# Local and global attention with an expert layer: smaller load pieces, weight buffers of their own, masks by half rows, global scores in spare columns

## The chip, the cores and the metric

The kernel runs on one core of a Trainium2 chip. The time is the device time of one execution in microseconds; it is given as the median of several runs, and one further execution is taken with the hardware profiler.

## What is computed

Eight batches of attention with 8 heads of size 64, 512 local and 32 global positions, and then a layer that replaces 128 chosen rows of each batch. All data is float32.

```python
k_all = concat([k_g, k_l]); v_all = concat([v_g, v_l])
out_g = softmax(q_g @ k_all.T / 8) @ v_all              # 32 global queries see everything
s_ll  = where(|i - j| <= 32, q_l @ k_l.T / 8, -1e9)     # local queries: a band
out_l = softmax([q_l @ k_g.T / 8, s_ll]) @ [v_g, v_l]   # and the 32 global keys
x = concat([out_g, out_l])                              # 8 batches, 576 rows, 512 wide
scores = x @ w_gate                                     # one number for each row
top = the 128 rows of each batch with the highest scores
x[top] += sigmoid(scores[top]) * (relu(x[top] @ w1) @ w2)    # w1 512x1024, w2 1024x512
```

## The kernel before

**Steps.** A batch is six steps in the order L0, L1, G0, L2, G1, L3. An L step is 128 local queries of all heads, a G step one half of the keys for the 32 global queries. Queries and keys lie with the head's 64 values along the partitions, two heads on top of each other, and the keys of a local block are 128 columns: two of its own, one global block, one neighbour. One loop (line 709) goes over all 48 steps as a software pipeline, so that in iteration `i` TensorE (PE) does, in this order: the mask of step `i+1` (`opened`, L247), the products with the values of step `i-1` (`attend_mm`, L328, or L429 for G), what stands in the list `early` (below), the scores of step `i+1` (L266, or L387), the transposes of step `i`'s exponentials (`transp`, L308 or L303), and then a share of the expert layer. ScalarE (ACT) takes exponentials (L293) and copies the transposes from PSUM (L315, tile `pt`), VectorE (DVE) does maxima and divisions. All engines follow the order in which the program is written.

**Mask.** `opened` takes one of three two-bank PSUM tiles `s_ps` and writes the mask into it before the scores are added: for each of the two banks one bfloat16 product of a 128x128 identity and 128 rows of mask, 256 columns. Such a pair stands in each of the 32 L steps.

**Global scores.** After the last G step of a batch `g_score` (L466) sums four partial scores of each global row by a one-column product, and DVE copies the 32 sums. One step later `spread_g` (L477) turns them into a row, which ACT copies into the tile `r` (L478 to L485), and `spread` (L484) does so for the 512 local scores. All three are called from `early` and take their PSUM tile from `m_tile()`, which hands out two buffers `m_ps` in turn. The expert layer takes its tiles from there too: L541 turns the gathered rows, L574 is the first product, L586 turns its result (copied by ACT and DVE into `hTh` and `hTl`, L589 and L590), L603 is the second product, whose tile stays open over four pieces of work.

**Loads.** Every load is issued by SyncE (SP) through `put` (L116). `put` counts back over the loads issued before it, and once their sizes with its own pass `UNDER` = 2000 KB, it makes the new load wait for the one at which this happened. So no more than 2000 KB are under way. Of each batch there are 4 pieces of keys of 416 KB, 8 of values of 520 KB, 2 of queries of 512 KB and a small one. The 16 pieces of expert weights (256 KB each) come in between by the table `LOADW` (iteration: number) and go into the buffers `xe` (shared with the rows that the expert layer gathers), `ws`, `xTh`, `xTl`, `hTh`, `hTl`, which the expert layer needs later. By the table `SPLITS` each piece is split into a rounded part (DVE for w1, ACT for w2) and a remainder (GpSimd). The expert layer begins at iteration 12.

Of the kernel before, what the change touches and what calls it, by code (L numbers as in the profile page):

```python
# [7 lines left out]
FP32 = mybir.dt.float32  # L8
# [9 lines left out]
P = 128  # L18
B, H, SL, SG, D = 8, 8, 512, 32, 64
ST = SG + SL  # L20
DM = H * D
FF = 1024
NT = SL // P
NC = SL // 32
NPAIR = H // 2
# [4 lines left out]
KC = DM // P  # L30
MC = FF // P
NEG = -1.0e30
# [4 lines left out]
ORDER = (("L", 0), ("L", 1), ("G", 0), ("L", 2), ("G", 1), ("L", 3))  # L37
PER = len(ORDER)
RESTL, LATE = 2, 6
LOADW = {4: 4, 5: 4, 7: 5, 11: 3}  # L40
SPLITS = {9: 2, 10: 3, 11: 3, 13: 3, 14: 3, 15: 2}

GROUPS = ((0,), (1,), (2,), (3,), (4,), (5,), (6,), (7,))
FIRST = 12
APART = 12
RANKS0 = {1: 2, 2: 3}
RANKS = {1: 1, 2: 2, 3: 2}
UNDER = 2000

RATE, HELD, FILL = 2.05, 2.6, 2.6  # L50
LEFT = 2.7
# [19 lines left out]
def kernel(ctx, tc, qT, kT, qgT, vw, w1, w2, wg, wgg, const, edge, outs, cap):  # L71
# [17 lines left out]

    ne = edge.shape[1] - P  # L90
    cb = cst.tile([P, ne], BF16, name="cb")
    ident16 = cb[:, 0:P]
    mask = cb[:, P:].rearrange("p (a k) -> p a k", a=3)
    ident = cs[:, o:o + P]; o += P
    slot = cs[:, o:o + NST * P]; o += NST * P
    tokid = cs[:, o:o + NT + 1]; o += NT + 1
# [10 lines left out]

    loaded = {}
    under = []

    def put(out, in_):
        kb = 4
        for n in in_.shape:
            kb *= n
        kb //= 1024
        d_ = nc.sync.dma_start(out=out, in_=in_)  # L116
        sum_ = kb
        for e_, k_ in reversed(under):
            sum_ += k_
            if sum_ > UNDER:  # L120
                tc.add_manual_dep(d_.ins, e_.ins.name, mybir.DependencyInfo(mybir.DependencyClass.Sync, mybir.DependencyReason.DATA), reason="under")
                break
        under.append((d_, kb))
        return d_
# [5 lines left out]
        loaded[b] = (q_t, k_t, qg_t)  # L130

    def load_q(b, n):
        put(out=loaded[b][0][n], in_=qT[b, n])

    def load_k(b, pr):
        put(out=loaded[b][1][:, pr], in_=kT[b, :, pr])
# [32 lines left out]

    def load_v(b, t):  # L170
        vts[b, t] = vld.tile([P, 4, H, VD], FP32, name="v_t")
        for j in range(0, 4, 2):
            put(out=vts[b, t][:, j:j + 2], in_=vw[b, t, :, j:j + 2])

    end = {"on": False, "n": 0}

# [1 line left out]
    def m_tile():  # L178
        if end["on"]:
            end["n"] += 1  # L180
            if end["n"] % 5 in (0, 1, 3):
                return ps_s.tile([P, 2, 512], FP32, name="s_ps")[:, 0]
        return ps_m.tile([P, 512], FP32, name="m_ps")
# [18 lines left out]
    raw = {}  # L202

    def load_w(k):
        if k < 4 or 12 <= k:
            raw[k] = moe.tile([P, DM], FP32, name="xe", bufs=5)
        elif k < 6:
            raw[k] = wst.tile([P, DM], FP32, name="ws")
        elif k < 8:
            raw[k] = moe.tile([P, DM], FP32, name=("xTh", "xTl")[k - 6])  # L210
        else:
            if k % 2 == 0:
                raw["t"] = moe.tile([P, 2, DM], FP32, name=("hTh", "hTl")[k // 2 - 4])
            raw[k] = raw["t"][:, k % 2]
        src = w1[:, k // 2, DM * (k % 2):DM * (k % 2) + DM] if k < 2 * KC else w2[:, k - 2 * KC]
        put(out=raw[k], in_=src)

# [21 lines left out]
    def opened(g):  # L239
        b, kind, t = g  # L240
        s_ps = ps_s.tile([P, 2, 512], FP32, name="s_ps")
        if kind == "G":
            return s_ps
        m = mask[:, 0 if t == 0 else (2 if t == NT - 1 else 1)]
        for hp in range(2):
            o_ = s_ps[:, hp]
            nc.tensor.matmul(  # L247
                out=bass.AP(tensor=o_.tensor, offset=o_.offset, ap=[o_.ap[0], [P, NPAIR], [P - 32, 2], [1, 32]]),
                lhsT=ident16,
                rhs=bass.AP(tensor=m.tensor, offset=m.offset, ap=[m.ap[0], [0, NPAIR], [1, 64]]),  # L250
                start=True, stop=False, skip_group_check=True)
        return s_ps
# [107 lines left out]
    def run_stores():  # L360
        while due:
            due.pop(0)()
        due.extend(stores)
        stores.clear()
# [96 lines left out]

    gs = {}

    def g_score(b):
        f_ps = m_tile()
        nc.tensor.matmul(out=f_ps[0:SG, 0:1], lhsT=fold, rhs=gs[b], start=True, stop=True)  # L466
        nc.vector.tensor_copy(out=sc[b][0:SG, NT:NT + 1], in_=f_ps[0:SG, 0:1])

# [2 lines left out]
    def spread_g(b):  # L471
        cnt = sm.tile([P, NT + 1], FP32, name="cnt")
        nc.vector.memset(cnt, 0.0)
        r = moe.tile([P, ST], FP32, name="r")
        rk[b] = (r, cnt)
        g_ps = m_tile()[:, 0:SG]
        nc.tensor.transpose(g_ps, sc[b][0:SG, NT:NT + 1].broadcast_to([SG, P]), ident[0:SG, 0:SG])  # L477
        nc.scalar.copy(out=r[:, SL:ST], in_=g_ps)  # L478

# [31 lines left out]
    def gather(b, s):  # L511
        ix_ps = m_tile()
        for i in range(NT + 1):
            n = P if i < NT else SG
            nc.tensor.matmul(out=ix_ps[:, 0:1], lhsT=oh[b][0:n, i, s * P:s * P + P], rhs=tok16[0:n, i:i + 1],
                             start=(i == 0), stop=(i == NT))
        ix = sm.tile([P, 1], U32, name="ix", bufs=4)
        nc.vector.tensor_copy(out=ix, in_=ix_ps[:, 0:1])
        xe = moe.tile([P, DM], FP32, name="xe", bufs=5)
        moves.append(lambda: nc.gpsimd.indirect_dma_start(  # L520
            out=xe, out_offset=None, in_=outs[b],
            in_offset=bass.IndirectOffsetOnAxis(ap=ix, axis=0),
        ))
        items[b, s] = (ix, xe)
# [174 lines left out]
        put(out=side[:, SL:SL + P], in_=edge[:, ne:ne + P])  # L699

    load_first()
    wl = list(range(2 * KC + MC))
    wload = list(wl)
    S, MX, PR, PT = {}, {}, {}, {}
    S[0] = opened(work[0])
# [3 lines left out]
    for i in range(nstep + 1):  # L709
        end["on"] = i >= nstep - 1  # L710
        b, s = divmod(i, PER)
        run_stores()
        if i < nstep:
            if b + 1 < B:
                if s == 0:
                    load(b + 1)
                    load_q(b + 1, 0)
                    load_k(b + 1, 0)
                    load_k(b + 1, 1)
                if s == 1:  # L720
                    load_k(b + 1, 2)
                    load_k(b + 1, 3)
                    load_v(b + 1, 0)
                if s == 3:
                    load_v(b + 1, 1)
                    load_qg(b + 1)
                if s == 4:
                    load_q(b + 1, 1)
                    load_v(b + 1, 2)
                if s == 5:  # L730
                    load_v(b + 1, 3)
            if i == RESTL:
                load_rest()
            for _ in range(LOADW.get(i, 0)):
                load_w(wload.pop(0))
        if i + 1 < nstep:
            S[i + 1] = opened(work[i + 1])
        if i > 0:
            attend_mm(work[i - 1], PT.pop(i - 1), S[i - 1])
        while early:  # L740
            fn, a = early.pop(0)
            fn(*a)
        if i + 1 < nstep:
            scores(work[i + 1], S[i + 1])
        if i < nstep:
            TP = transp(work[i], PR.pop(i), S[i], i < APART)
        if i > 0:
            attend_out(work[i - 1], S.pop(i - 1))
        if i + 1 < nstep:
            MX[i + 1] = maxima(work[i + 1], S[i + 1])  # L750
        if i > 0 and work[i - 1][1] == "L":
            finish(work[i - 1][0], work[i - 1][2])
        if i < nstep:
            PT[i] = turned(work[i], TP)
        if i + 1 < nstep:
            PR[i + 1] = expo(work[i + 1], S[i + 1], MX.pop(i + 1))
        if i == nstep:
            run_stores()
            run_stores()
        if i == LATE:  # L760
            nc.vector.tensor_copy(out=tok16, in_=tokid)
            nc.vector.tensor_copy(out=slot16, in_=slot)
        for _ in range(SPLITS.get(i, 0)):
            split(wl.pop(0))
        if i < nstep and s == 0 and b > 0:
            early.append((spread_g, (b - 1,)))
            chains.append(chain(b - 1))
        if s == 5 and i < nstep:
            early.append((g_score, (b,)))
        run_chains(i)  # L770
        if i < nstep:
            have = sum(f[0] for f in fill)
            if groups[0][0] < B - 1:
                run_fill(RATE)
            else:
                run_fill(max(0.0, min((have - LEFT) / (nstep - i), FILL)))
        run_moves()
# [27 lines left out]
def _layout(inputs):  # L805
# [25 lines left out]
    for c in range(NC):  # L831
# [10 lines left out]
        f["moe_w_gate"].reshape(4, 1, 2 * D), (4, SG, 2 * D)).reshape(P, 2 * D))  # L842

    j = np.arange(32)
    m = np.zeros((3, P, 2, 32), np.float32)
    m[:, :, 0] = np.tile(np.where(j[None, :] >= j[:, None], 0.0, NEG), (4, 1))
    m[:, :, 1] = np.tile(np.where(j[None, :] <= j[:, None], 0.0, NEG), (4, 1))
    m[0, 0:32, 0] = NEG
    m[2, 96:128, 1] = NEG
    ii = np.arange(P)  # L850
    edge = np.concatenate([np.eye(P, dtype=np.float32), m.transpose(1, 0, 2, 3).reshape(P, -1),
                           np.where(ii[None, :] >= ii[:, None], TINY, 0.0).astype(np.float32)], axis=1)
    tok = np.empty((P, NT + 1), np.float32)
    for t in range(NT):
# [38 lines left out]
```

## Time and profile before

| | |
|---|---|
| median of 3 runs | 334.17 us (333.85 to 334.65) |
| the profiled execution: its time | 334.12 us |
| its span, first to last instruction | 332.1 us |
| mean granted TensorE clock | 0.961 |
| busy: PE, PE's weight loads, DVE, ACT, GpSimd | 280.8, 217.7, 192.0, 179.3, 39.1 us |
| instructions of PE: products, weight loads | 6248, 6248 |
| data moved | 75.42 MB, 227 GB/s over the span |

Busy time is the sum of an engine's instructions and is not a bound by itself: PE works 85% of the span, and what matters is what ends the rest. The profiled execution lies 0.05 us from the median, so sums made against it can be read against the median. In the trace "issue" is time in which an engine waited for nothing that the profile shows.

### The profile page before, as it was taken

What the parts mean: (1) busy time and instruction counts of PE and PEld (TensorE: products, weight loads), DVE (VectorE), ACT (ScalarE), POOL (GpSimd) and SP (SyncE); (2) the same over time, 40 slices, a digit from 0 to 9 for tenths busy, and PEclk for the clock granted to TensorE, in tenths of its full rate; (3) what the DMA queues carried; (4) which work ended last, traced back from release to release, by engine and by line L of the source; (5) the groups of instructions that cost most, each with busy time, mean ns of one, the idle gap of its engine ahead of it and who ended that gap; (6) DMA issues with size and microseconds to landing.
All of it is one profiled execution on the core that took longest, in us unless ns stands there. A gap on an engine that the chain in (4) does not pass through costs nothing.

```text
span 332.1 us, 14114 instructions
## 1 busy us (share of the span) xinstructions
PE 280.8 (85%) x6248; PEld 217.7 (66%) x6248; DVE 192.0 (58%) x477; ACT 179.3 (54%) x563; POOL 39.1 (12%) x41
## 2 busy tenths in 40 slices
PE   7976577686998899879998999969989899959993
PEld 3654465564877677667776777757766677748882
DVE  0553528596578657555764577553863667636412
ACT  1766457266687657447666564736647465611220
POOL 2000000463353100010001001000001001101111
PEclk9999979698999999999999999989999999969998
DMA  7999998999999996696398818893385002020100
GB/s 231 380 297 383 322 322 247 368 338 302 325 372 341 329 355 204 209 335 262 105 350 271 338 56 266 286 366 96 126 326 174 34 36 98 19 88 32 34 32 32
DMA packets 29900, 75.42 MB, mean 227 GB/s; under 512 B 3216, under 2 KB 8848, under 8 KB 29840
## 3 DMA queue, kind: packets, MB, share of 16 engines
q1 hardware_dynamic: 22608, 61.27, 53.4%
q10 hardware_dynamic: 5952, 9.06, 7.6%
q0 software_dynamic: 1280, 4.20, 3.5%
q8 instruction: 49, 0.80, 1.0%
q14 instruction: 11, 0.09, 0.1%
HBM read 63.51 MB, written 11.01 MB: 224 GB/s over the span
## 4 chain that ended last, share of the span: by engine, by line
issue 40%; PE 24%; ACT 12%; DMA 11%; DVE 8%; POOL 2%; POOLq 1%; ACTq 0%; SPq 0%
ACT p_t L293 6%; PE s_ps L308 4%; PE s_ps L266 4%; PE m_ps L603 4%; DMA q_t<-in_qT_dram 4%; PE s_ps L328 4%; DMA v_t<-in_vw_dram 3%; DMA k_t<-in_kT_dram 3%; PE m_ps L574 3%; ACT pt L315 3%; DVE mxl L280 2%; DMA out_dram<-ogs 1%; ACT pg L411 1%; POOL out_dram L610 1%; DVE junk L492 1%
## 5 line engine op out<-in xcount | busy, mean ns | idle before, releaser
L315 ACT COPY pt<-s_ps 128x512 f32<-128x512 f32 (+1 forms) x72 | 36.1, 554 | 64.2 <-PE s_ps L308 41.0
L293 ACT ACTIVATE p_t<-s_ps,nb 128x128 f32<-128x128 f32 x256 | 69.5, 383 | 1.0
L328 PE MATMUL s_ps<-v_t,pt 128*32 128x65 f32 x2048 | 41.0, 226 | 12.8 <-issue 9.1
L328 PEld LDWEIGHTS s_ps<-v_t,pt 128*32 128x32 f32 x2048 | 33.7, 112 | 22.9 <-issue 14.8
L280 DVE TENSOR_REDUCE mxl<-s_ps 128x8 f32<-128x1024 f32 x32 | 39.0, 1218 | 13.4 <-PE s_ps L266 13.4
L266 PE MATMUL s_ps<-k_t,q_t 64*32 64x128 f32 x2048 | 40.9, 285 | 5.1 <-issue 2.6
L266 PEld LDWEIGHTS s_ps<-k_t,q_t 64*32 64x32 f32 x2048 | 30.5, 109 | 9.7 <-issue 6.6
L492 DVE SCALAR_TENSOR_TENSOR junk<-r,sc,side 128x544 bf16<-128x544 f32 (+1 forms) x40 | 31.2, 781 | 5.3 <-ACT r L485 3.1
L308 PE MATMUL s_ps<-cs,p_t 128*128 128x128 f32 x192 | 28.0, 291 | 3.3 <-ACT p_t L293 2.9
L603 PE MATMUL m_ps<-w2h,hTh 128*128 128x512 f32 x64 | 28.6, 446 | 0.1
L308 PEld LDWEIGHTS s_ps<-cs,p_t 128*128 128x128 f32 x192 | 21.9, 147 | 9.4 <-ACT p_t L293 5.9
L342 DVE TENSOR_SCALAR den<-s_ps 128x8 f32<-128x8 f32 x32 | 5.1, 158 | 38.4 <-PE s_ps L328 36.0
L603 PE MATMUL m_ps<-w2l,hTh 128*128 128x512 f32 x64 | 26.2, 409 | 0.0
L315 ACT COPY pt<-m_ps 128x512 f32<-128x512 f32 (+1 forms) x24 | 12.4, 556 | 22.0 <-PE m_ps L303 11.3
L574 PE MATMUL m_ps<-w1h,xTh 128*128 128x512 f32 x56 | 23.4, 417 | 0.0
L368 DVE CUSTOM_DVE_ANT_0 junk<-x,wgb 128x512 bf16<-128x512 f32 x32 | 23.1, 723 | 0.0
L348 DVE TENSOR_TENSOR x<-s_ps,rec 128x512 f32<-128x512 f32 x32 | 22.1, 691 | 1.1
L610 POOL DMA_INDIRECT out_dram<-xe,ix x8 | 8.2, 1026 | 123.2 <-DVE ga L440 87.2
L590 DVE TENSOR_TENSOR hTl<-m_ps,hTh 128x512 fp32r<-128x512 f32 x11 | 7.6, 692 | 25.5 <-ACT hTh L589 23.5
L574 PE MATMUL m_ps<-w1l,xTh 128*128 128x512 f32 x56 | 22.0, 392 | 0.0
L429 PE MATMUL s_ps<-v_t,pt 128*32 128x65 f32 x768 | 15.7, 224 | 7.2 <-issue 3.6
L411 ACT ACTIVATE pg<-s_ps,nbg 128x64 f32<-128x64 f32 (+2 forms) x80 | 21.1, 357 | 0.6
(115 smaller groups left out, 431.6 us busy)
## 6 DMA issues: line engine op xcount, KB each, us to landing
v_t<-in_vw_dram SPq DMA_DIRECT2D x64, 520.0 KB
k_t<-in_kT_dram SPq DMA_DIRECT2D x28, 416.0 KB
out_dram<-x ACTq DMA_DIRECT2D x32, 256.0 KB
q_t<-in_qT_dram SPq DMA_DIRECT2D x15, 512.0 KB
xe<-in_w_dram SPq DMA_DIRECT2D x8, 256.0 KB
k_t<-in_kT_dram SPq DMA_DIRECT2D x3, 384.0 KB
k_t<-in_kT_dram SPq DMA_DIRECT2D x1, 512.0 KB
q_t<-in_qT_dram SPq DMA_DIRECT2D x2, 256.0 KB
```

Of the source, the lines that this page charges most:

```text
L266: nc.tensor.matmul(out=s_ps[32 * j:32 * j + 32, hp, P * pr:P * pr + P], lhsT=q_t[t // 2][rows, pr, 32 * (c % 8):32 * (c % 8) + 32], rhs=wi ...
L280: nc.vector.tensor_reduce(out=mx, in_=s_ps.rearrange("p a (r k) -> p (a r) k", k=P), axis=AX.X, op=ALU.max)
L293: nc.scalar.activation(out=p_t[hp][:, cc], in_=s_ps[:, hp, cc], func=AF.Exp, scale=0.125, bias=nb[:, k:k + 1])
L308: nc.tensor.transpose(t_ps[hp][:, cc], p_t[hp][:, cc], ident)
L315: nc.scalar.copy(out=pt[hp][:, 0:n], in_=t_ps[hp][:, 0:n])
L328: nc.tensor.matmul(out=s_ps[32 * j:32 * j + 32, hp, VD * pr:VD * pr + VD], lhsT=pt[hp][:, x0:x0 + 32], rhs=v_t[:, j, NPAIR * hp + pr, :], ...
L348: nc.vector.tensor_tensor(out=xt[b, t].rearrange("p r a d -> p a r d"), in0=o_ps[:, :, :, 0:D], in1=rec.broadcast_to([P, 2, NPAIR, D]), op ...
L368: nc.vector.tensor_tensor_reduce(out=junk[:n, 0:DM], in0=xf, in1=wgb[:n], op0=ALU.mult, op1=ALU.add, scale=1.0, scalar=0.0, accum_out=dst,)
L411: nc.scalar.activation(out=bass.AP(tensor=d_.tensor, offset=d_.offset, ap=[d_.ap[0], [4 * 32, n], [1, 32 * ln]]), in_=bass.AP(tensor=s_.te ...
L492: nc.vector.scalar_tensor_tensor(out=junk[:n], in0=r[:n], scalar=sc[b][0:n, i:i + 1], in1=side[:n, x0:x0 + ST], op0=ALU.subtract, op1=ALU. ...
L574: nc.tensor.matmul(out=hs["p"], lhsT=xT[x_][:, kc, 0:P], rhs=a[:, kc, fs], start=(part == 0 and i == 0), stop=(part == 1 and i == len(prod ...
L603: nc.tensor.matmul(out=y_ps, lhsT=hT[h_][:, mc, cc], rhs=w[:, mc, :], start=(part == 0 and i == 0), stop=(part == 3 and i == len(prods) - 1))
```

## The change

Five things change. (1) Queries and values come in pieces of 256 and 260 KB, and the bound on the data under way is 1700 KB in iterations 0 to 11 and 1500 KB afterwards. (2) The weights have four buffers `raw` of their own, `xe` has three instead of five, and the pieces come in another order and at other iterations, as do their splits; the gathered rows no longer share buffers with weights. (3) The mask of each bank is one product over 64 rows instead of 128: the left operand `pick` chooses, row by row, between the inner mask and that of the first or last block, which stand in the two halves of the 64 rows; bank 0 takes rows 0 to 63, bank 1 rows 64 to 127. The constant `cb` grows from 80 to 112 KB. (4) `g_score` and `spread_g` write into the last 32 columns of the second bank of the `s_ps` tile of step `i-1`, which is then still in use for that step, instead of a tile from `m_tile()`. (5) The scratch memory for descriptors is set to 8192.

```diff
-LOADW = {4: 4, 5: 4, 7: 5, 11: 3}
-SPLITS = {9: 2, 10: 3, 11: 3, 13: 3, 14: 3, 15: 2}
+WORDER = (0, 2, 4, 6, 1, 3, 5, 7) + tuple(range(8, 16))
+LOADW = {5: 4, 7: 4, 9: 4, 14: 4}
+SPLITS = {10: 2, 11: 3, 12: 3, 13: 4, 16: 2, 17: 2}
...
-UNDER = 2000
+UNDER = (1700, 1500)
...
-    ident16 = cb[:, 0:P]
-    mask = cb[:, P:].rearrange("p (a k) -> p a k", a=3)
+    pick = cb[:, 0:2 * P].rearrange("p (a k) -> p a k", a=2)
+    mask = cb[:, 2 * P:].rearrange("p (a k) -> p a k", a=3)
...
-            if sum_ > UNDER:
+            if sum_ > limit["kb"]:
...
-        put(out=loaded[b][0][n], in_=qT[b, n])
+        for r in range(0, NPAIR, 2):
+            put(out=loaded[b][0][n][:, r:r + 2], in_=qT[b, n, :, r:r + 2])
...
-        for j in range(0, 4, 2):
-            put(out=vts[b, t][:, j:j + 2], in_=vw[b, t, :, j:j + 2])
+        for j in range(4):
+            put(out=vts[b, t][:, j], in_=vw[b, t, :, j])
...
-        if k < 4 or 12 <= k:
-            raw[k] = moe.tile([P, DM], FP32, name="xe", bufs=5)
-        elif k < 6:
+        n = WORDER.index(k)
+        if n < 2:
+            raw[k] = moe.tile([P, DM], FP32, name=("xTh", "xTl")[n])
+        elif n < 4:
             raw[k] = wst.tile([P, DM], FP32, name="ws")
-        elif k < 8:
-            raw[k] = moe.tile([P, DM], FP32, name=("xTh", "xTl")[k - 6])
+        elif n < 8 or n >= 12:
+            raw[k] = moe.tile([P, DM], FP32, name="raw", bufs=4)
...
-        m = mask[:, 0 if t == 0 else (2 if t == NT - 1 else 1)]
+        v = 0 if t == 0 else (2 if t == NT - 1 else 1)
         for hp in range(2):
-            o_ = s_ps[:, hp]
+            rows = slice(D * hp, D * hp + D)
+            o_, m = s_ps[:, hp], mask[rows, v]
...
-                lhsT=ident16,
+                lhsT=pick[rows, v // 2],
...
+    def small():
+        return spare["t"][:, 1, 512 - SG:512] if spare["t"] is not None else m_tile()[:, 0:SG]
+
     def g_score(b):
-        f_ps = m_tile()
+        f_ps = small()
...
-        g_ps = m_tile()[:, 0:SG]
+        g_ps = small()
...
-        xe = moe.tile([P, DM], FP32, name="xe", bufs=5)
+        xe = moe.tile([P, DM], FP32, name="xe", bufs=3)
...
+        limit["kb"] = UNDER[i >= 2 * PER]
...
+        spare["t"] = S.get(i - 1)
         while early:
             fn, a = early.pop(0)
             fn(*a)
+        spare["t"] = None
```

On TensorE, around `g_score` of the fourth batch and the `spread_g` that follows it (`pt` is the turned exponentials, `gs` the partial scores, `sc` the scores of a batch, `cs` constants), before:

```order
L328 MATMUL s_ps<-v_t,pt_2728 32x65 x16
L466 MATMUL m_ps<-gs,cs 32x1
L266 MATMUL s_ps<-k_t,q_t 32x128 x32
...
L328 MATMUL s_ps<-v_t,pt_2857 32x65 x16
L477 MATMUL m_ps<-cs,sc 128x32
L484 MATMUL m_ps<-cs,sc 128x128 x4
L387 MATMUL s_ps<-k_t,qg_t 32x256 x8
```

and now:

```order
L333 MATMUL s_ps<-v_t,pt_2771 32x65 x16
L476 MATMUL s_ps<-gs,cs 32x1
L271 MATMUL s_ps<-k_t,q_t 32x128 x32
...
L333 MATMUL s_ps<-v_t,pt_2900 32x65 x16
L487 MATMUL s_ps<-cs,sc 128x32
L494 MATMUL m_ps<-cs,sc 128x128 x4
L392 MATMUL s_ps<-k_t,qg_t 32x256 x8
```

The instructions stand in the same places; the one-column product and the small transpose go to `s_ps`, and the four transposes behind them stay in `m_ps`.

On SP, the loads of iterations 4 to 6 (`v_t` values, `q_t` queries, `k_t` keys, and weights into `xe`, `ws`, `xTh`, `xTl`), before:

```order
L116 DMA q_t<-in_qT_dram 128x1024
L116 DMA v_t<-in_vw_dram 128x1040 x2
L116 DMA xe<-in_w_dram 128x512 x4
L116 DMA v_t<-in_vw_dram 128x1040 x2
L116 DMA ws<-in_w_dram 128x512 x2
L116 DMA xTh<-in_w_dram 128x512
L116 DMA xTl<-in_w_dram 128x512
L116 DMA q_t<-in_qT_dram 128x1024
L116 DMA k_t<-in_kT_dram 128x832 x4
```

and now:

```order
L118 DMA q_t<-in_qT_dram 128x512 x2
L118 DMA v_t<-in_vw_dram 128x520 x8
L118 DMA xTh<-in_w_dram 128x512
L118 DMA xTl<-in_w_dram 128x512
L118 DMA ws<-in_w_dram 128x512 x2
L118 DMA q_t<-in_qT_dram 128x512 x2
L118 DMA k_t<-in_kT_dram 128x832 x4
```

The values no longer stand behind four pieces of weights, and queries and values are twice as many loads of half the size; the order of keys, queries and values among themselves is as before.

## Rows read from the trace of the kernel before

**Rows 1.** Stretches: window in us, its length, busy us, clock, DMA share, GB/s.

```profile
core 0: us, PE busy (x) PEld busy (x) DVE busy (x) ACT busy (x) POOL busy (x), PEclk, DMA share, GB/s
34.00:95.00 61.00, 46.17 (x1217) 35.86 (x1225) 39.09 (x91) 35.82 (x115) 15.98 (x13) 0.89 0.94 322
91.30:99.60 8.30, 8.16 (x166) 5.92 (x172) 6.16 (x15) 7.38 (x23) 4.41 (x4) 1.00 1.02 369
99.60:108.00 8.40, 7.17 (x207) 5.96 (x203) 7.24 (x18) 6.07 (x18) 2.50 (x2) 1.00 0.96 343
257.00:290.00 33.00, 30.12 (x692) 24.25 (x692) 21.66 (x57) 19.73 (x61) 1.96 (x2) 1.00 0.13 45
```

**Rows 2.** Waits of PE: line and what it waited for, total us, times, longest.

```profile
PE s_ps L328 <- issue: 9.1, 10, 2.0
PE m_ps L466 <- DVE hTl L590: 4.7, 4, 1.5
PE m_ps L308 <- issue: 3.7, 1, 3.7
PE s_ps L429 <- issue: 3.6, 4, 1.5
...
PE s_ps L328 <- ACT pt L315: 3.3, 6, 0.7
...
PE s_ps L266 <- issue: 2.6, 2, 1.5
...
PE m_ps L484 <- ACT r L478: 1.4, 5, 0.3
...
PE s_ps L266 <- DMA k_t<-in_kT_dram: 1.3, 2, 0.8
```

**Rows 3.** The page's list of DMA queues: packets, MB, share of time.

```profile
q8 instruction: 49, 0.80, 1.0%
```

**Rows 4.** Timeline of PE, 34 to 46 us: start, us, instruction, [idle before].

```profile
34.17 0.45 PE L266 MATMUL s_ps<-k_t,q_t 64*32 64x128 f32 x16 [0.52 <-DMA k_t<-in_kT_dram]
...
37.62 1.06 PE L328 MATMUL s_ps<-v_t,pt 128*32 128x65 f32 x58 [1.43 <-issue]
...
43.81 1.65 PE L308 MATMUL m_ps<-cs,p_t 128*128 128x128 f32 x7 [3.73 <-issue]
```

**Rows 5.** Timeline of PE at products of L466 and L484.

```profile
146.95 0.22 PE L466 MATMUL m_ps<-gs,cs 128*32 128x1 f32 x2 [1.29 <-DVE hTl L590]
...
153.55 0.65 PE L484 MATMUL m_ps<-cs,sc 128*128 128x128 f32 x4 [0.28 <-ACT r L478]
...
182.22 0.22 PE L466 MATMUL m_ps<-gs,cs 128*32 128x1 f32 x2 [0.96 <-DVE hTl L590]
...
258.24 0.22 PE L466 MATMUL m_ps<-gs,cs 128*32 128x1 f32 x2 [1.45 <-DVE hTl L590]
```

**Rows 6.** Timeline of PE at issue waits after 95 us.

```profile
104.19 0.31 PE L429 MATMUL s_ps<-v_t,pt 128*32 128x65 f32 x4 [0.93 <-issue]
...
184.68 0.33 PE L308 MATMUL s_ps<-cs,p_t 128*128 128x128 f32 x1 [0.24 <-issue]
...
220.62 0.43 PE L266 MATMUL s_ps<-k_t,q_t 64*32 64x128 f32 x11 [1.46 <-issue]
...
246.90 0.66 PE L303 MATMUL s_ps<-cs,pg 128*128 128x128 f32 x4 [1.40 <-issue]
```

**Rows 7.** Timeline of PE around a mask, and at a step without one.

```profile
86.98 0.62 PE L574 MATMUL m_ps<-w1h,xTl 128*128 128x512 f32 x2
87.44 0.39 PE L247 MATMUL s_ps<-cb 128*128 128x256 bf16 x2
87.77 0.44 PE L328 MATMUL s_ps<-v_t,pt 128*32 128x65 f32 x16
...
284.02 0.62 PE L574 MATMUL m_ps<-w1h,xTl 128*128 128x512 f32 x2
284.57 0.89 PE L429 MATMUL s_ps<-v_t,pt 128*32 128x65 f32 x48
```

**Rows 8.** Timeline of SP from 42 us.

```profile
41.99 3.14 SPq L116 DMA_DIRECT2D xe<-in_w_dram  x4
```

More of the change, by code (lines that the diff above doesn't have):

```diff
@@ L109 @@
     under = []
+    limit = {"kb": UNDER[0]}
     def put(out, in_):
@@ L204, in load_w @@
     def load_w(k):
-        if k < 4 or 12 <= k:
-            raw[k] = moe.tile([P, DM], FP32, name="xe", bufs=5)
-        elif k < 6:
+        n = WORDER.index(k)
+        if n < 2:
+            raw[k] = moe.tile([P, DM], FP32, name=("xTh", "xTl")[n])
+        elif n < 4:
             raw[k] = wst.tile([P, DM], FP32, name="ws")
-        elif k < 8:
-            raw[k] = moe.tile([P, DM], FP32, name=("xTh", "xTl")[k - 6])
-        else:
-            if k % 2 == 0:
-                raw["t"] = moe.tile([P, 2, DM], FP32, name=("hTh", "hTl")[k // 2 - 4])
-            raw[k] = raw["t"][:, k % 2]
+        elif n < 8 or n >= 12:
+            raw[k] = moe.tile([P, DM], FP32, name="raw", bufs=4)
+        else:
+            if n % 2 == 0:
+                raw["t"] = moe.tile([P, 2, DM], FP32, name=("hTh", "hTl")[n // 2 - 4])
+            raw[k] = raw["t"][:, n % 2]
         src = w1[:, k // 2, DM * (k % 2):DM * (k % 2) + DM] if k < 2 * KC else w2[:, k - 2 * KC]
@@ L462 @@
     gs = {}
+    spare = {"t": None}
+    def small():
+        return spare["t"][:, 1, 512 - SG:512] if spare["t"] is not None else m_tile()[:, 0:SG]
     def g_score(b):
-        f_ps = m_tile()
+        f_ps = small()
         nc.tensor.matmul(out=f_ps[0:SG, 0:1], lhsT=fold, rhs=gs[b], start=True, stop=True)
@@ L701 @@
     load_first()
-    wl = list(range(2 * KC + MC))
+    wl = list(WORDER)
     wload = list(wl)
@@ L844, in _layout @@
     j = np.arange(32)
[L845 to L849, printed above, removed]
-    ii = np.arange(P)
-    edge = np.concatenate([np.eye(P, dtype=np.float32), m.transpose(1, 0, 2, 3).reshape(P, -1),
+    prev = np.where(j[None, :] >= j[:, None], 0.0, NEG)
+    nxt = np.where(j[None, :] <= j[:, None], 0.0, NEG)
+    out = np.full((32, 32), NEG)
+    mid, first, last = (np.stack(a, axis=1) for a in ((prev, nxt), (out, nxt), (prev, out)))
+    m = np.stack([np.tile(np.concatenate([mid, e]), (2, 1, 1)) for e in (first, mid, last)], axis=1)
+    ii = np.arange(P)
+    pick = np.zeros((2, 2, 2, 32, P), np.float32)
+    for v, edge_block in enumerate((0, P // 32 - 1)):
+        at_edge = (ii // 32 == edge_block).astype(int)
+        pick[v, :, at_edge, ii % 32, ii] = 1.0
+    edge = np.concatenate([pick.reshape(2, P, P).transpose(1, 0, 2).reshape(P, -1), m.reshape(P, -1),
                            np.where(ii[None, :] >= ii[:, None], TINY, 0.0).astype(np.float32)], axis=1)
@@ L878 @@
     laid, cap = _layout(inputs)
-    nc = _bacc.Bacc("TRN2", target_bir_lowering=False, num_devices=1)
+    nc = _bacc.Bacc("TRN2", target_bir_lowering=False, num_devices=1, dynamic_dma_scratch_size=8192)
     arrays, args = {}, []
```

## The prediction

> **What bounds the kernel now.** I read the page's busy shares first: PE works 85% of the span, no other engine more than 58%. So the time is PE's work plus PE's waits, and an edit is worth what it takes from one of the two. Then I read the waits of PE, and the stretches for what the loads do meanwhile.
>
> The largest waits have no releaser: "issue", 9.1 + 3.7 + 3.6 + 2.6 us in the four long rows [rows 2], and with two of 1.40 and 0.24 [rows 6] 20.6 us in all. They stand in the middle of runs of equal products: after four value products, PE pauses for 1.43 us and goes on with 58 more of them; after one transpose it pauses for 3.73 us and goes on with seven [rows 4]. No data can be late there. What fits is the fetch of instructions: queue q8 moved 49 packets of together 0.80 MB [rows 3], 16 KB each, and PE's 2 x 6248 instructions make 255 to a packet. I take these waits for late fetches. They are long where loads run (3.73 us in a stretch with a DMA share of 0.94), and after 246.90 [rows 6] there is none in the 33 us from 257 us on, where that share is 0.13 [rows 1]. So a fetch seems to queue behind the loads that are under way.
>
> The second largest is L466 behind `hTl`, 4.7 us in 4 waits [rows 2]: the one-column product of the global scores wants a buffer `m_ps` that DVE is still reading for the expert layer. Loads are waited for as such in little: the keys for 1.3 us in two waits [rows 2], one of them 0.52 us at 34.17 [rows 4], though the DMA engines are busy 0.94 of the time from 34 to 95 us [rows 1].
>
> **The change part by part**, summed against the profiled execution of 334.1 us, which the median of 334.17 us equals.
>
> *Global scores in spare columns.* L466 and L477 stay where they are and lose the claim on `m_ps`. The columns that they write belong to step `i-1`, whose turned exponentials ACT has copied out before `attend_mm` could start, so nothing new is waited for. Of the four waits, 1.29 and 1.45 us [rows 5] go fully: -2.7. The other two (0.96 at 182.22 [rows 5], and what is left of 4.7) are each followed by an issue wait 2.5 us later, at 184.68 and 220.62 [rows 6]. If PE is there earlier it waits longer for the same fetch; I count nothing for them here. If the fetch moves along, they are worth another 1.9. The freed rotation also ends the 0.28 us that L484 waits for ACT's copy of the small transpose [rows 2, 5]: 5 waits, 1.4 us. One lies before 95 us, where fetches swallow such gains; four count, -1.1. What is late next is the ordinary latency of ACT: the copy `pt` costs PE 3.3 us in 6 waits already [rows 2].
>
> *Masks.* Today the two products of a mask begin 0.33 us before the value products behind them, and the two products ahead of them take 0.46 us (86.98 to 87.44); where no mask stands between, the same two are followed after 0.55 us (284.02 to 284.57) [rows 7]. So there is a loss of 0.55 - 0.46 = 0.09 us when PE goes from 128-row, 128-column tiles to tiles of 32 columns, and a mask pair costs 0.33 - 0.09 = 0.24. Two products on different row halves can lie beside each other, as the score products of two heads do: 0.12. But the tile form now changes once more ahead of the mask, +0.09. That makes 0.46 + 0.09 + 0.12 + 0.09 = 0.76 against 0.79 us: -0.03 x 32 pairs = -1.0. Bounds: no loss at the extra change, -0.12 x 32 = -3.8; products not beside each other, +0.09 x 32 = +2.9. I take the middle, because the row shows the loss at exactly such a change. The Trainium skill ("TensorEngine Tiling (Array Packing)", Key Properties) says that a change of tiling mode, not of the tile alone, drains TensorE; the trace agrees with 0.09 us. By that rule alone, without the gain of lying side by side, the part would be the +2.9.
>
> *Pieces and bound, after 95 us.* With 2000 KB and pieces of 520 KB three are under way, 1560 KB; with 1500 KB and 260 KB five, 1300 KB. As the oldest piece is half moved on average, the mean falls from 1300 to 1170 KB. At 343 GB/s (99.6 to 108 us [rows 1]) the 130 KB are 0.4 us of queue ahead of a fetch; the full 260 KB would be 0.8. There are seven issue waits after 95 us (the first and last of 0.93 and 1.40 [rows 6]); five of them are 0.9 us or longer, and with the one at 184.68, which will have grown by the removed L466 wait, six can use it: 6 x -0.4 = -2.4. Bounds 0 and -4.8.
>
> *Pieces and bound, 34 to 95 us.* Here 1700 KB hold six pieces, 1560 KB as before, but the mean is 1430 KB instead of 1300, +0.4 us for a fetch that falls among queries and values. Where weights of 256 KB load, as at the wait of 3.73 us (SP issues four of them from 41.99 us [rows 8]), seven were allowed and now six are, 256 KB less: up to -0.8. Of about nine waits I put six to the first and one to the second: +2.4 - 0.8, rounded to +1.5. Bounds -2.5 and +3.6.
>
> SP issues 220 loads instead of 141. At the 3.14 / 4 = 0.79 us that it took for one with its waits [rows 8], 220 are 174 us of 332: SP has room, and an issue ends long before its data is wanted.
>
> *Weights.* The loads of a w2 piece and its ACT cast come later, from iterations 14 and 15 to 16 and 17, and the GpSimd queue now issues the gather ahead of remainders instead of behind them. In 91.30 to 99.60, where two of these steps lie, PE is busy 8.16 of 8.30 us, and in the next stretch 7.17 of 8.40, ACT 6.07 [rows 1]: PE's work hides the casts today, and it would have to cover them 1.2 us poorer later on. I count 0, and +-1.5 as bounds, the wait that one cast pair in the wrong place makes between an exponential and its transpose. The larger constant `cb` is 32 KB, 0.1 us at the start, uncounted.
>
> Sum: -2.7 - 1.1 - 1.0 - 2.4 + 1.5 = -5.7, that is **328.4 us**.
>
> **The rivals.**
>
> *A. The fetch hangs on the size of a piece or its packets, not on the bytes under way.* Then halving the pieces halves all 20.6 us of issue waits: -2.7 - 1.1 - 1.0 - 10.3 = -15.1, 319.0 us. For it: these waits are long only where loads run. Against it: the longest stands where 256 KB pieces load already [rows 4, 8]. The Trainium skill ("DMA: Bandwidth & Descriptors", Queues, rings and completion order) says that a DMA engine alternates between queues packet by packet; by that a fetch would wait for one packet and not for everything under way. The rows of 1.4 to 3.7 us do not look like one packet.
>
> *B. Small pieces move slower, and the loads become the bound (the slower side).* Place: 0 to 95 us, where the DMA share is 0.94 [rows 1] and nothing is in reserve. If the rate falls by 15%, 95 us of loading become 112, +16.8, and the time is 334.1 - 7.2 + 16.8 = 343.7 us. It decides when the rate falls by more than 7%, 7.2 / (95 + 7.2). For it: the share of 0.94, and half as many bytes in each row of a piece. Against it: the 256 KB weights run today in the same stretches at 322 GB/s, the bytes under way are the same 1560 KB, and only 0.52 us of PE is lost to keys there [rows 4]. The Trainium skill ("DMA: Bandwidth & Descriptors", Bandwidth) asks for transfers of 1 MiB and more for three quarters of the peak; no row here has one of that size, and the 322 GB/s are reached with a quarter and half of it.
>
> *C. The waits removed come back elsewhere.* PE's next stop behind L466 and L484 is the scores and transposes, and ACT's chain (maximum, exponential, copy) sets when these may run. If that chain sets the step, PE waits for `pt` (3.3 us today [rows 2]) instead. Then of 2.7 + 1.1 only 0.5 is left, the masks give 1.0 and the fetches nothing: 332.6 us. For it: PE is busy 85%, with ACT and DVE in a loop with it. Against it: the 1.29 and 1.45 us are stops of PE while ACT and DVE have the step ahead still to do with PE's products.
>
> **How the numbers follow.** The forecast has a chance of 0.53, A 0.08, C 0.21, B 0.18. The forecast's own range, from the bounds of masks, fetches and weights taken together as independent, is 324 to 332. I leave out A (0.08) and the part of B above 336 us (0.11) and get 322.5 to 336. A measurement of this kernel can tell about 0.2%, 0.7 us, from no change. Faster by more: 0.50 of the forecast, A, and 0.15 of C, whose 332.6 lies only 1.5 us below: 0.73. Within: 0.02 of the forecast, 0.04 of C, 0.02 of B: 0.08. Slower: 0.16 of B, 0.02 of C and 0.01 of the forecast: 0.19.
>
> **What the changed profile would show.** The row of L466 behind `hTl` is gone (it would be L476), and with it that of L484 behind `r`; no wait of these products on ACT takes their place. The time from the last L574 before a mask to the first value product behind it is 0.76 us; at 0.67 the extra change of tile form costs nothing, at 0.88 the halves don't overlap. Issue waits after 95 us sum to some 2.4 us less, and those before it to about as much as today; if both halve, it is A. The stretch of 34 to 95 us keeps 320 GB/s; if it falls below 300 and rows of PE behind `k_t`, `q_t` or `v_t` appear, it is B. The prediction would be wrong above all if issue waits are not fetches behind loads, or if the loads fall behind.

## The result

| | before | after |
|---|---|---|
| median of 4 runs | 334.41 us (333.85 to 334.94) | 322.65 us (321.06 to 323.78) |
| ratio, 95% interval | | 0.9645 (0.9592 to 0.9699) |
| profiled execution, span | 334.12, 332.1 us | 323.78, 321.8 us |
| mean granted TensorE clock | 0.961 | 0.943 |
| PE busy | 280.8 us | 278.5 us |

The kernel became 11.8 us faster, 3.5%; 328.4 had been forecast, 5.7 faster, with a range down to 322.5. On the three chips used below single executions of the kernel before lie 3 to 4% apart (medians 333.0, 332.4 and 333.0 us), so the ratios, their intervals and the differences in us worked out from them come from undisturbed runs alone, while a median beside them is that of all runs and the profiled executions of e2, e3, e6 and e7 are disturbed ones.

The waits of PE in the changed kernel (line and what it waited for, total us, times, longest), which answer to [rows 2]:

```profile
PE s_ps L271 <- DMA k_t<-in_kT_dram: 5.4, 6, 1.5
PE s_ps L271 <- issue: 3.8, 4, 2.7
PE m_ps L525 <- DVE hTl L600: 3.7, 1, 3.7
PE s_ps L434 <- issue: 3.3, 3, 2.2
...
PE s_ps L333 <- ACT pt L320: 2.4, 5, 0.7
...
PE s_ps L333 <- issue: 1.1, 3, 0.6
...
PE m_ps L584 <- issue: 0.6, 1, 0.6
PE s_ps L313 <- issue: 0.3, 1, 0.3
```

The one-column product of the global scores is L476 now and the four transposes behind it L494: neither has a row of waits. The issue rows sum to 9.1 us, from 20.6. Against that, keys are waited for 5.4 us instead of 1.3, and one wait of 3.7 us has come up at L525, the products that turn ranks into indices. By stretch, as in [rows 1]:

```profile
34.00:95.00 61.00, 51.18 (x1397) 39.99 (x1401) 41.65 (x100) 38.91 (x123) 17.33 (x13) 0.87 0.96 326
...
99.60:108.00 8.40, 4.39 (x30) 3.50 (x21) 3.77 (x12) 3.68 (x10) 2.49 (x2) 0.76 0.99 337
```

From 34 to 95 us the loads run as before (326 against 322 GB/s) and PE is busy 51.2 instead of 46.2 us, with 1397 products instead of 1217. From 99.6 to 108 us it is busy 4.4 instead of 7.2 us, at a clock of 0.76 instead of 1.00: a loss inside the gain. (The products of one stretch are partly others before and after, so their numbers alone say less.)

The mask on the timeline of PE, as in [rows 7]:

```profile
82.09 0.63 PE L584 MATMUL m_ps<-w1h,xTl 128*128 128x512 f32 x2
82.65 0.28 PE L252 MATMUL s_ps<-cb 64*128 64x256 bf16 x2
82.86 1.14 PE L333 MATMUL s_ps<-v_t,pt 128*32 128x65 f32 x64
```

From the first of the two L584 to the value products it takes 0.77 us; it took 0.79, and 0.76 was forecast.

### The profile page after: what moved, and what is told of

It is laid out like the page before. It is cut to its first block, busy times and chain, and to the rows that moved or that the text cites. A ratio compares the mean times of both kernels' runs of the same rounds, so it can differ in the third digit from the quotient of the medians.

```text
span 321.8 us, 14200 instructions
## 1 busy us (share of the span) xinstructions
PE 278.5 (87%) x6248; PEld 216.4 (67%) x6248; DVE 189.6 (59%) x477; ACT 179.3 (56%) x563; POOL 39.7 (12%) x41
## 4 chain that ended last, share of the span: by engine, by line
DMA 32%; PE 27%; issue 26%; SPq 5%; ACT 4%; DVE 3%; POOL 2%; POOLq 0%; ACTq 0%; DVEq 0%
DMA k_t<-in_kT_dram 14%; DMA v_t<-in_vw_dram 8%; PE m_ps L613 5%; SPq L118 5%; PE m_ps L584 5%; PE s_ps L333 4%; DMA q_t<-in_qT_dram 4%; PE s_ps L271 4%; DMA raw<-in_w_dram 3%; PE s_ps L313 2%; DMA out_dram<-ogs 2%; PE s_ps L308 2%; DMA hTh<-in_w_dram 2%; PE s_ps L434 1%; POOL out_dram L620 1%
## 5 line engine op out<-in xcount | busy, mean ns | idle before, releaser
L271 PE MATMUL s_ps<-k_t,q_t 64*32 64x128 f32 x2048 | 42.2, 289 | 10.4 <-DMA k_t<-in_kT_dram 5.4
L333 PE MATMUL s_ps<-v_t,pt 128*32 128x65 f32 x2048 | 38.8, 227 | 3.6 <-ACT pt L320 2.4
L333 PEld LDWEIGHTS s_ps<-v_t,pt 128*32 128x32 f32 x2048 | 32.7, 113 | 10.4 <-ACT pt L320 4.1
L502 DVE SCALAR_TENSOR_TENSOR junk<-r,sc,side 128x544 bf16<-128x544 f32 (+1 forms) x40 | 32.1, 804 | 4.9 <-ACT r L495 2.8
L600 DVE TENSOR_TENSOR hTl<-m_ps,hTh 128x512 fp32r<-128x512 f32 x15 | 10.4, 692 | 38.0 <-ACT hTh L599 38.0
L313 PE MATMUL s_ps<-cs,p_t 128*128 128x128 f32 x192 | 26.4, 280 | 2.1 <-ACT p_t L298 1.7
L313 PEld LDWEIGHTS s_ps<-cs,p_t 128*128 128x128 f32 x192 | 20.6, 141 | 7.6 <-ACT p_t L298 4.2
L530 POOL DMA_INDIRECT xe<-out_dram,ix x8 | 7.9, 987 | 135.3 <-DVE ix L528 135.2
L434 PE MATMUL s_ps<-v_t,pt 128*32 128x65 f32 x768 | 15.1, 223 | 10.5 <-issue 3.3
L613 PE MATMUL m_ps<-w2h,hTh 128*128 128x512 f32 x48 | 22.7, 472 | 0.8 <-DVE gs L462 0.8
L373 DVE CUSTOM_DVE_ANT_0 junk<-x,wgb 128x512 bf16<-128x512 f32 x32 | 22.5, 702 | 0.0
L434 PEld LDWEIGHTS s_ps<-v_t,pt 128*32 128x32 f32 x768 | 12.1, 110 | 15.0 <-issue 8.5
L584 PE MATMUL m_ps<-w1h,xTh 128*128 128x512 f32 x52 | 21.6, 416 | 0.6 <-issue 0.6
```

The costliest lines, as they stand in the source:

```text
L271: nc.tensor.matmul(out=s_ps[32 * j:32 * j + 32, hp, P * pr:P * pr + P], lhsT=q_t[t // 2][rows, pr, 32 * (c % 8):32 * (c % 8) + 32], rhs=wi ...
L313: nc.tensor.transpose(t_ps[hp][:, cc], p_t[hp][:, cc], ident)
L333: nc.tensor.matmul(out=s_ps[32 * j:32 * j + 32, hp, VD * pr:VD * pr + VD], lhsT=pt[hp][:, x0:x0 + 32], rhs=v_t[:, j, NPAIR * hp + pr, :], ...
L373: nc.vector.tensor_tensor_reduce(out=junk[:n, 0:DM], in0=xf, in1=wgb[:n], op0=ALU.mult, op1=ALU.add, scale=1.0, scalar=0.0, accum_out=dst,)
L434: nc.tensor.matmul(out=s_ps[32 * pr:32 * pr + 32, hp, 0:VD], lhsT=ptg[hp][:, P * i + 32 * pr:P * i + 32 * pr + 32], rhs=vts[b, c // 4][:, ...
L502: nc.vector.scalar_tensor_tensor(out=junk[:n], in0=r[:n], scalar=sc[b][0:n, i:i + 1], in1=side[:n, x0:x0 + ST], op0=ALU.subtract, op1=ALU. ...
```

## Experiments

"The kernel before plus one part" is meant unless something else is said. "Issue" is the sum of PE's issue rows in the one profiled execution, "keys" the median time from issue to landing of a 416 KB piece of keys, which every kernel loads in the same form; the page of the kernel before gives none, and r12 loads none.

| run | median us, before on that chip | ratio, 95% interval | issue us | keys us |
|---|---|---|---|---|
| e1_spare | 325.30, 333.00 | 0.985 (0.977 to 0.992) | 22.5 | 6.2 |
| e2_mask | 332.93, 333.00 | 1.000 (0.994 to 1.006) | 26.5 | 6.3 |
| e3_pieces_2000 | 325.63, 333.00 | 0.976 (0.966 to 0.987) | 13.8 | 6.2 |
| e4_pieces_bound | 330.30, 333.00 | 1.002 (0.997 to 1.008) | 10.1 | 5.2 |
| e5_rows2080 | 335.09, 332.36 | 1.002 (0.997 to 1.008) | 19.3 | 6.1 |
| e6_halves | 376.28, 332.36 | none given | 31.0 | 6.9 |
| e7_bound1400 | 354.85, 332.36 | 1.069 (1.062 to 1.076) | 7.9 | 4.3 |
| e8_weights | 333.71, 332.36 | 1.007 (1.003 to 1.012) | 16.3 | 6.6 |
| r9_after | 321.44, 332.97 | 0.970 (0.963 to 0.978) | 7.5 | 5.7 |
| r10_after_2000 | 318.91, 332.97 | 0.963 (0.956 to 0.971) | 18.0 | 7.2 |
| r11_spare_pieces | 317.51, 332.97 | 0.959 (0.951 to 0.967) | 11.7 | 7.1 |
| r12_no_loads | 318.83 (2 runs), 332.97 | none given | 5.7 | |

The traces also hold the start and the end of each packet of the instruction queue q8. Counted over PE's products and weight loads in the order of their starts, the issue waits stand at instruction 193 or 194 and every 256 instructions behind it: all of them in these runs and in the changed kernel, and 19.6 of the 20.6 us before. PE goes on 1.1 to 1.8 us after the end of a packet; at the wait of 3.73 us in [rows 4] the packet ran from 41.59 to 42.55 us, and PE went on at 43.81. So PE waits there for its next 256 instructions. Such a group is called a block below, and its fetch is said to begin when the next packet does.

**e1_spare**, the global scores alone.

```diff
-        f_ps = m_tile()
+        f_ps = small()
...
-        g_ps = m_tile()[:, 0:SG]
+        g_ps = small()
```

> The kernel before with the global scores in spare columns and nothing else. If removed waits count where they stand: the 4.7 us row of the one-column product behind hTl and the 1.4 us row behind r vanish, and the time falls by 2.7 + 1.1 = 3.8 us, to about 330.5. If they come back elsewhere (rival C): under 1 us, 333.5 or more, with rows behind pt or behind another reader of m_ps as much longer.

The ratio times 333 is 5.0 us, the interval 2.5 to 7.6, so the forecast 3.8 lies inside it. PE's timeline of this kernel at four of the places of [rows 5, 6]:

```profile
141.22 0.20 PE L471 MATMUL s_ps<-gs,cs 128*32 128x1 f32 x2
...
175.22 0.20 PE L471 MATMUL s_ps<-gs,cs 128*32 128x1 f32 x2
...
179.28 0.38 PE L308 MATMUL s_ps<-cs,p_t 128*128 128x128 f32 x2 [1.97 <-issue]
...
215.52 0.44 PE L266 MATMUL s_ps<-k_t,q_t 64*32 64x128 f32 x11 [2.30 <-issue]
```

L471 waits for DVE nowhere (its one wait is 0.5 us for a constant at the start). But the fetch that PE waited 0.24 us for at 184.68 now costs 1.97, and the one at 220.62 2.30 instead of 1.46: what is taken out between the start of a block and its end is spent waiting for the next one, as the forecast had it. The first of these fetches begins 2.6 us after the start of its block in both kernels. Rival C is not what happened: the row behind `pt` is 3.3 us as before.

**e2_mask**, the 64-row products alone (the lines of `opened`, `pick` and `mask` in the diff of the change).

> The kernel before with the 64-row mask products and nothing else. With one more change of tile form at 0.09 us and the halves side by side: 0.76 us from the last L574 to the first value product (0.79 before), and 1.0 us less, 333.3. If the extra change costs nothing, 0.67 us and 3.8 less; if the halves don't overlap, 0.88 us and 2.9 more.

Nothing measurable (the interval is 2.0 us to either side). Its timeline shows 0.77 and 0.78 us, as the changed kernel does; 32 times 0.02 is 0.6 us, below what the runs can tell. The halves do overlap (two products begin and end in 0.28 us): the pair begins 0.21 us before the value products instead of 0.33. But it begins 0.56 instead of 0.46 us after the products ahead of it, and that one more change of tile form costs what the gain is worth.

**e3_pieces_2000** and **e4_pieces_bound**, small pieces with the old bound and with the new ones.

```diff
-        put(out=loaded[b][0][n], in_=qT[b, n])
+        for r in range(0, NPAIR, 2):
+            put(out=loaded[b][0][n][:, r:r + 2], in_=qT[b, n, :, r:r + 2])
...
-        for j in range(0, 4, 2):
-            put(out=vts[b, t][:, j:j + 2], in_=vw[b, t, :, j:j + 2])
+        for j in range(4):
+            put(out=vts[b, t][:, j], in_=vw[b, t, :, j])
```

> The kernel before with queries and values in pieces of 256 and 260 KB, the bound still 2000 KB. If a fetch queues behind the bytes under way: seven pieces of 260 KB are 1820 KB, the mean 1690 instead of 1300, 390 KB or 1.1 us more per fetch at 343 GB/s; on the seventeen waits that can show it the issue rows grow from 20.6 to some 30 us or more, and the time is slower, 337 to 345. If the size of a piece sets the wait (rival A): issue rows near 10 us, and the time 324 to 328.

> The kernel before with the smaller pieces and the bounds of 1700 and 1500 KB. By bytes under way: 2.4 us less of issue waits after 95 us, 1.5 more before, the time 333 us, and clearly below the same pieces at 2000 KB. By the size of a piece: as with 2000 KB, 324 to 328, whatever the bound.

The pieces alone give 2.4%, 8.0 us (4.5 to 11.5), which my reckoning of bytes under way had as a loss. With the lower bounds the issue rows fall further, from 13.8 to 10.1, and yet the gain is gone. The waits of PE with the bounds:

```profile
PE m_ps L468 <- DVE hTl L592: 6.6, 4, 2.3
PE s_ps L268 <- DMA k_t<-in_kT_dram: 6.6, 8, 1.5
...
PE m_ps L486 <- ACT r L480: 2.7, 5, 1.6
...
PE s_ps L389 <- DMA qg_t<-in_qgT_dram: 1.6, 1, 1.6
```

With the old bound these are 5.2, 5.6, 1.5 and none: keys and other data come later, and so do the steps of DVE and ACT that PE waits for.

**e5_rows2080**, rows of half the length in pieces of the old size.

```diff
-        for j in range(0, 4, 2):
-            put(out=vts[b, t][:, j:j + 2], in_=vw[b, t, :, j:j + 2])
+        for j in range(2):
+            put(out=vts[b, t][:, j::2], in_=vw[b, t, :, j::2])
```

> The kernel before with value pieces that still hold 520 KB, but in rows of 2080 bytes (blocks 0 and 2, then 1 and 3) instead of 4160. If the length of a row sets the wait of a fetch: issue rows of PE fall from about 20 to about 13 us as with small pieces, 325 to 328. If the size of a piece or the bytes under way set it: issue rows stay at 20 us or more, 332 to 335.

Issue rows of 19.3 us and no gain: in pieces of 520 KB the length of a row is not it.

**e6_halves**, small pieces with rows of the old length.

```diff
-            put(out=vts[b, t][:, j:j + 2], in_=vw[b, t, :, j:j + 2])
+            for p in range(0, P, 64):
+                put(out=vts[b, t][p:p + 64, j:j + 2], in_=vw[b, t, p:p + 64, j:j + 2])
```

> The kernel before with pieces of 256 and 260 KB made of 64 partitions instead of 128, so that the rows keep 4096 and 4160 bytes, bound 2000 KB. If the size of a piece sets the wait: issue rows near 13 us and 325 to 328 as with the other small pieces. If the length of a row sets it, or the bytes under way: issue rows of 20 us or more, 332 to 338.

This doesn't answer its question, since another thing came first: the loads slowed down. The stretches:

```profile
0.00:34.00 34.00, 24.55 (x591) 17.25 (x592) 10.23 (x23) 15.63 (x50) 2.30 (x9) 0.80 0.97 246
34.00:95.00 61.00, 37.35 (x1025) 26.96 (x1029) 32.46 (x79) 27.28 (x90) 11.80 (x9) 0.78 0.96 261
```

Here the kernel is bound by its loads, as in rival B, with 18.5 us of waits for keys, and the issue rows are larger than in any other run.

**e7_bound1400**, two large pieces under way instead of three (`UNDER = 1400`).

> The kernel before with a bound of 1400 instead of 2000 KB: two pieces of 520 KB are under way instead of three, 520 KB less. If the bytes under way set the wait: up to 1.5 us less for each fetch in a loaded stretch, issue rows near 8 us, and the time falls by up to 10 us as far as the loads keep up; their rate would fall and rows of PE behind k_t and v_t grow. If the size or rows of a piece set it: issue rows of 20 us as before, and the time no better than 333.

Issue rows and loads came as expected, and the time is 6.9% longer. Keys land after 4.3 instead of 6.2 us (e1, with the loads of the kernel before) and the issue rows shrink to 7.9 us; but from 34 to 95 us only 274 GB/s are left, and PE waits 20.0 us for keys. So this run says little about fetches: while PE stands at keys, its next instructions have time to land, and from 95 to 200 us the fetches begin on average 2.1 us after the start of a block, as in the kernel before (2.1).

**e8_weights**, the weights' buffers, order, loads and splits, and the scratch memory (those lines of the diff).

> The kernel before with the weights' own buffers, order, loads and splits and nothing else. The forecast's 0 with bounds of 1.5 us: 331.5 to 334.5. If the casts on ACT collide in iterations 16 and 17, p_t and pt rows of PE grow by 1 to 2 us; if the shared buffers held loads or the gather back before, the wait for the gathered rows (3.4 us) and k_t shrink.

A loss of 0.9 to 3.9 us (the interval times 332.4) where nothing to 1.5 had been reckoned; the wait for the gathered rows stays at 3.5 us, so the shared buffers had not held the gather up.

**r9_after** and **r10_after_2000**, the changed kernel on this chip, and with `UNDER = (2000, 2000)`.

> The changed kernel itself once more, on the chip of the other three, as the measure for them: 0.96 to 0.97 of the kernel before.

> The changed kernel with the bound put back to 2000 KB. If the lower bounds cost more in late keys than they give in fetches, as the two runs with small pieces alone say (330.3 against 325.6): about 4 us below the changed kernel, 318 to 320, with k_t rows of PE a little smaller and issue rows a few us larger. If the bounds serve the whole change (by bytes under way a lower bound should shorten fetches): 2 to 5 us above it, with issue rows of 13 us or more instead of 9.

The old bound is better by 2.5 us (0.963 against 0.970), and five of its six runs lie below the fastest of the changed kernel; the intervals overlap, so the size is uncertain. The issue rows grow by 10.5 us (7.5 to 18.0) and still the kernel is faster. Keys are waited for 2.3 instead of 5.7 us (r9), and a second gain is seen on ACT. The changed kernel, then r10:

```profile
102.09 0.62 ACT L232 CAST w2h<-raw 128x512 fp32r<-128x512 f32 x1 [2.08 <-DMA raw<-in_w_dram]
...
103.48 0.58 ACT L599 CAST hTh<-m_ps 128x512 fp32r<-128x512 f32 x1
```

```profile
96.97 1.19 ACT L232 CAST w2h<-raw 128x512 fp32r<-128x512 f32 x2
97.99 0.65 ACT L599 CAST hTh<-m_ps 128x512 fp32r<-128x512 f32 x1
```

ACT stands in the queue at the cast of a w2 piece that has not landed. Behind it waits `hTh`, then DVE's `hTl`, then PE:

```profile
104.84 0.36 PE L525 MATMUL m_ps<-tok,oh 128*128 128x1 f16 x5 [3.68 <-DVE hTl L600]
```

With the bound of 2000 the piece is there. In r9 the same cast waits 1.96 us. After the pause PE's clock is lower; the stretch right behind it in the changed kernel:

```profile
104.80:108.00 3.20, 3.16 (x12) 2.58 (x12) 3.06 (x11) 0.80 (x4) 0.48 (x1) 0.50 0.99 342
```

The granted clock of 0.50 is the level of 1.2 GHz; in the kernel before it is 1.00 in these 3.2 us. The products of w2 in 99 to 112 us in the changed kernel, and in the kernel before:

```profile
L613 PE MATMUL m_ps<-w2h,hTh 128*128 128x512 f32 x4 | 2.7, 673 | 0.0
```

```profile
L603 PE MATMUL m_ps<-w2h,hTh 128*128 128x512 f32 x4 | 1.7, 420 | 0.0
```

**r11_spare_pieces**, spare columns and small pieces at 2000 KB, and no other part of the change: the diffs of e1 and e3 together.

> The kernel before with spare columns and small pieces at 2000 KB, and neither masks, weights nor bounds. If the two parts add up: 7.7 + 7.4 us below the kernel before, about 318. If both take the same time, since PE that comes earlier waits longer for a fetch: no better than 324.

They add up: 13.7 us (11.1 to 16.3), where the two alone gave 5.0 and 8.0. It has the lowest median here; all six of its runs (316.25 to 319.72 us) lie below the fastest of the changed kernel (320.28), though the intervals overlap at the edge. So masks, weights and bounds together cost about 4 us (13.7 against the 9.9 of r9), some 2.5 of it the bounds (r10).

**r12_no_loads.**

```diff
-                    load(b + 1)
-                    load_q(b + 1, 0)
...
+                loaded[b + 1] = loaded[0]
+                for t in range(NT):
+                    vts[b + 1, t] = vts[0, t]
```

> The kernel before without the loads of batches 1 to 7: every batch computes with the queries, keys and values of batch 0, so the other seven batches of the output are those of batch 0. If the issue waits are fetches behind loads: they all but vanish after the last weights (some 45 us), to below 3 us in sum from 20, while PE's instructions stay the same, and the time falls to 300 to 310. If they belong to the instructions themselves or to the 16 KB of a fetch: they stay at some 15 to 20 us.

Its issue waits, all of them:

```profile
13.65 0.69 PE L387 MATMUL s_ps<-k_t,qg_t 64*32 64x256 f32 x23 [0.25 <-issue]
...
19.78 0.84 PE L266 MATMUL s_ps<-k_t,q_t 64*32 64x128 f32 x35 [0.83 <-issue]
...
32.13 1.53 PE L429 MATMUL s_ps<-v_t,pt 128*32 128x65 f32 x48 [3.95 <-issue]
...
49.72 0.49 PE L429 MATMUL s_ps<-v_t,pt 128*32 128x65 f32 x20 [0.52 <-issue]
...
58.89 0.32 PE L429 MATMUL s_ps<-v_t,pt 128*32 128x65 f32 x7 [0.23 <-issue]
```

None after 59 us: with nothing to load, PE's instructions arrive in time, though it runs the same ones. From 34 to 95 us a fetch begins on average 1.1 us after the start of its block, and 3.2 in the kernel before. That is the direct evidence for the reading on which the prediction rested. The time missed its 300 to 310 us (315.99 and 321.66 in two runs): the issue waits gave back 14.9 us, and other waits stay, those of L466 behind `hTl` with 6.8 us among them.

## Why the prediction was right, and where its steps failed

**The reading of the profile held.** Issue waits are fetches of instructions behind loads: they stand 256 instructions apart, end behind a packet of q8, and all but vanish without loads (r12). They are shorter with lower bounds (e4, r9 and the changed kernel), where keys land sooner too: after 6.1 to 7.2 us at 2000 KB, 5.1 to 5.7 at 1700 and then 1500, and 4.3 at 1400 KB (e7).

**Global scores, -3.8.** The mechanism was right, down to the fetch that swallows one gain at 184.68. There the wait grew by 1.73 us, more than the 0.96 taken out; at 220.62 by 0.84 for 0.97. Measured 5.0 us, 2.5 to 7.6 by the interval, so nothing beyond the removed rows is shown. One profiled execution has more or less issue waits by several us without any change to its loads (20.6 to 26.5 us in before, e1 and e2).

**Masks, -1.0.** Right: 0.77 for 0.76 us, -0.6, and no difference that the runs could tell. The rule on the change of tiling mode ("TensorEngine Tiling (Array Packing)" in the Trainium skill, Key Properties) holds here with some 0.1 us for each change, and by that price the gain of two overlapping halves is eaten up.

**Pieces and bounds after 95 us, -2.4.** The issue waits there fell from 8.1 to 5.7 us, which is the forecast. I had counted seven such waits, and there are ten; the three more, 0.34 to 0.38 us each, stand at no block's end. The 0.4 us for a fetch are not shown: from 95 to 200 us a fetch begins 2.1 us after the start of its block before, and 2.0 and 2.1 us in the changed kernel (its two traces). So the right sum is in part luck.

**Pieces and bounds from 34 to 95 us, +1.5: the step that failed.** I reckoned the mean under way from the bound less half a piece, 1430 KB instead of 1300, and put 0.4 us more on each fetch, for about nine waits (there are seven). The fetches of this stretch come sooner instead, 2.7 and 2.4 us after the start of a block (changed kernel, r9) instead of 3.2, and its issue waits fell from 10.9 to 3.1 us. What is under way is not by itself the measure of a fetch's wait: with the bound unchanged, keys of this stretch land later with small pieces (5.8, 6.6 and 7.3 us in e3, r11 and r10) than with large ones (5.2 in e1), and yet fetches begin no later (2.7, 2.5 and 2.9 us; 3.3 in e1). Over the whole run small pieces shorten the issue rows from a mean of 19.7 us (before, e1, e5, e8) to 14.9 (r10, r11), and lower bounds to 8.9 (e4, r9 and the changed kernel), where some of it may be that PE stands at keys while a fetch is on its way. Why pieces of half the size do so at one bound isn't settled; rows of half the length alone do nothing (e5).

**Rival A** (0.08) came nearest in what the issue rows do, halved as it said. At one bound the size of a piece does count (e3, r11), and that bounds count as well is not in it. Rival B did not decide at 1700 and 1500 KB, but its place and sign were right: every lower bound was paid for with later loads, the whole gain of the pieces in e4.

**Weights, 0 with bounds of 1.5: under-sized.** e8 lost 2.4 us (0.9 to 3.9). What costs it there is not shown: no cast on ACT waits for a piece, and L468 waits 6.4 instead of 4.7 us behind `hTl`. The mechanism that was named, a cast in the wrong place on ACT, shows only with the lower bounds (2.08 us in the changed kernel, 1.96 in r9, none in e8 and r10). I had checked PE's cover at the old place and not whether the piece would have landed at the new one.

So the sum came out too small by half. The range held, but 322.65 us lies only 0.15 us inside its end, and two of the four executions (321.06 and 321.65) lie below it, so that it held is luck. Besides the sign of one term it was adding the parts that failed. Measured alone, the four parts as the change has them give -5.0 (e1), 0.0 (e2), +0.8 (e4) and +2.4 us (e8), -1.8 in sum, and together -9.9 (r9), more than the intervals allow. Lower bounds lengthen just the waits that spare columns remove: L468 and L486 wait 6.6 and 2.7 us in e4, against 4.7 and 1.4 in their rows before, and neither row is left in the changed kernel. That is 3.2 of the 8.1 us; the rest stays open. Spare columns and small pieces at 2000 KB do add up (r11), and they alone give some 4 us more than the whole change.

## What to carry to other kernels

When an engine pauses in the middle of equal instructions with no releaser, set its number of instructions against the packets of the instruction queue, and see whether the pauses stand one packet's instructions apart. If they do and fall where loads run, smaller pieces are worth trying before a lower bound, which pays for earlier fetches with later data. A gain between the start of a block and such a wait is lost again unless the fetch moves with it. Parts that remove and add the same wait do not add up, so measure them together too. Before moving work on a queue that runs in order, look whether its operand has landed at the new place, because everything behind it waits too.

## What the runs showed of the hardware that was not expected

- PE's instructions came in packets of 16 KB, one for 256 products and weight loads. With loads running (34 to 95 us) a packet began on average 3.2 us after the start of a block, without them (r12) 1.1; PE went on 1.1 to 1.8 us after its end.
- Pieces of 64 partitions with rows of 4 KB moved at 246 and 261 GB/s (e6), where pieces of 128 partitions with the same bytes moved at 333 and 334 (e3). The fastest of the six runs took 367.3 us, against a median of 332.4 before.
- Pieces of 260 KB ran at 326 GB/s and pieces of 520 KB at 322 (34 to 95 us): no loss from halving them here.
- A pause of 3.7 us on PE was followed by 3.2 us at a granted clock of 0.50, the level of 1.2 GHz, and products of w2 took 673 instead of 420 ns: the wait cost more than it lasted.
